# Loading wv and wq by rows, and splitting the first transposed copy between two engines

## The chip, the cores and the metric

The kernel runs on one core of one Trainium2 chip. A core has TensorE (matrix products; its weight loads are listed apart), VectorE, ScalarE, GpSimd, and SyncE (SP), whose queue issues the transfers that sixteen DMA engines carry out. In the profile they are PE, PEld, DVE, ACT, POOL and SP. The metric is device time in microseconds (us), lower is better.

## The reference

The input x has 2048 rows of 512 bf16 values; it is normalised by rows, and that xn feeds two branches:

```
xn  = layernorm(x)
qkv = xn @ wqkv                     # 512 x 1536: q, k and v, 32 heads of 16
s   = attention over 8 positions (pos, pos-2, ..., pos-14) of each head, then @ wo
h   = gelu(layernorm(xn) @ w1); its four column quarters shifted by +1, -1, +2, -2 rows; @ w2
x1  = xn + h
g   = silu(x1 + gelu(layernorm(x1) @ w3) @ w4)
out = x + s * g
```

`wqkv` is one matrix in memory, 1536 columns wide. Its columns 0 to 511 are wq, the next 512 wk, the last 512 wv. A row of one of these three parts is 1024 bytes long and lies 3072 bytes from the next row.

## The kernel before, in words

The rows are taken in two interleaved halves (even and odd rows), each as eight tiles of 128 rows; four tiles make a chunk of 512, so there are four chunks (0 to 3). The weights are held with 128 of their 512 input rows to a block, on the 128 partitions: index `dt` from 0 to 3 runs over these row blocks.

The order of work on each engine is the order of the program text; nothing is reordered, and engines wait for one another by semaphores. SP's queue is one list as well. Its first entries are, in this order: row tiles 0 and 1 (L105, 128 KB each), wv as one transfer (L114, 512 KB), row tiles 2 and 3 (L105), wq as two transfers of 256 of its 512 columns each (L118), wk (L121), then the tiles of chunk 1 two at a time (L105), w1 (L125), the tiles of chunk 2 (L105). A transfer in this list also waits until the one eight places before it has landed, because eight semaphores are used in turn.

The start, which the change touches, goes as follows. VectorE measures each row tile (L225, L227), ScalarE and VectorE make the inverse deviation (L232, L234), VectorE normalises the tile in place (L241). For chunk 0 TensorE then transposes the tiles. Tiles 0 and 1 go one at a time through `turn_one` (four 128 x 128 transposes each, L318, into one PSUM bank, which is copied to `xnT` at L320: tile 0 by VectorE, tile 1 by ScalarE). Tiles 2 and 3 go together through `turn` (L308, copied by VectorE at L309).

TensorE's list from there is: the v products of tiles 0 and 1 (`v_mm`, L380, four per tile, one for each row block of wv); the q products of tiles 0 and 1 for the first 256 columns of wq (`q_half`, L331, eight); the transposes of tiles 2 and 3 (L308); the q products of tiles 0 and 1 for the other 256 columns (eight); then the q products of tiles 2 and 3, eight and eight, with one product for the row factors of the second layer norm between them (`rows2_here`, L291); then k (`k_all`, L341 by way of `proj`), further v tiles, and w1 (L341). In `q_half` the loop over `nt` (four groups of 128 output columns) is the outer one and the loop over `dt` the inner one: a column group is finished before the next is begun. The four groups lie in four PSUM banks.

ScalarE, after tile 1's copy: the square roots for tiles 2 and 3 (L232), for the row factors (L259), the copy of v out of PSUM (L391), the load of another function table (L556, 1.28 us), the copy of the row factors (L292), the two copies of q (L352), then those of k (L371). Banks are used in pairs, three pairs in turn, and two single banks.

The rest is the second and third chunks' projections, w2, w3 (L489), and from about 108 us on an attention part in 18 steps, in which the products with w4 (L819) fill TensorE's list between the attention's own; it ends with the products with wo (L876) and the gates on VectorE (L891, L895).

Of the kernel before, what the change touches and what calls it, by code (L numbers as in the profile page):

```python
# [8 lines left out]
AF = mybir.ActivationFunctionType  # L9
# [11 lines left out]
def kernel(  # L21
# [17 lines left out]
    PE, DVE, ACT, POOL, SP = nc.tensor, nc.vector, nc.scalar, nc.gpsimd, nc.sync  # L39

    def pin(ins):

        return tc.keep_in_program_order(ins)
# [3 lines left out]
    D = 512  # L47
    F = 1376
    ND = D // P
# [20 lines left out]
    wqkv_v = A_wqkv.rearrange("(dt q) n -> q dt n", q=P)  # L70
# [14 lines left out]
    def b4(shape, name):  # L85
        return sm4.tile(shape, BF16, name=name, tag="b4")
# [4 lines left out]
    def pair():  # L91
        cnt["d"] += 1
        b = 2 * ((cnt["d"] - 1) % 3)
        return PS[:, b : b + 2, :]

    def single():
        cnt["s"] += 1
        return PS[:, 6 + (cnt["s"] - 1) % 2, :]
# [4 lines left out]
    def load_x(c, t0, n):  # L103
        p, i = c // 2, (c % 2) * TPC + t0
        pin(SP.dma_start(  # L105
            out=xn[p][:, i : i + n, :], in_=xv[p, i * P : (i + n) * P, :].rearrange("(i q) d -> q i d", q=P)
        ))

    wq_sb = b4([P, ND, D], "wq_sb")
    wk_sb = b4([P, ND, D], "wk_sb")  # L110
    wv_sb = b4([P, ND, D], "wv_sb")
    load_x(0, 0, 1)
    load_x(0, 1, 1)
    pin(SP.dma_start(out=wv_sb, in_=wqkv_v[:, :, 2 * D : 3 * D]))  # L114
    load_x(0, 2, 1)
    load_x(0, 3, 1)
    for h in range(2):
        pin(SP.dma_start(  # L118
            out=wq_sb[:, :, h * D // 2 : (h + 1) * D // 2], in_=wqkv_v[:, :, h * D // 2 : (h + 1) * D // 2]
        ))  # L120
    pin(SP.dma_start(out=wk_sb, in_=wqkv_v[:, :, D : 2 * D]))  # L121
    load_x(1, 0, 2)
    load_x(1, 2, 2)
# [186 lines left out]
            out=xnT[p][:, :, i * P : (i + 2) * P], in_=pt.rearrange("p a j q -> p a (j q)")  # L310
        ))

    def turn_one(c, t, eng):
        p, k = c // 2, c % 2
        i = k * TPC + t
        pt = single().bitcast(BF16)[:, 0 : ND * P].rearrange("p (a q) -> p a q", a=ND)
        for dt in range(ND):
            pin(PE.transpose(pt[:, dt, :], xn[p][:, i, dt * P : (dt + 1) * P], ident[:]))  # L318
        dst = xnT[p][:, :, i * P : (i + 1) * P]
        pin(DVE.tensor_copy(out=dst, in_=pt) if eng is DVE else ACT.activation(dst, pt, AF.Copy))  # L320

    def turn_dma(c, lo=0, hi=TPC):
        p, k = c // 2, c % 2
# [1 line left out]
            i = k * TPC + t  # L325
            pin(SP.dma_start_transpose(out=xnT[p][:, :, i * P : (i + 1) * P], in_=xn[p][:, i, :]))

    def q_half(pts, lo, hi, nts=range(ND)):
        for nt in nts:
            for dt in range(ND):  # L330
                pin(PE.matmul(  # L331
                    pts[nt // 2][:, nt % 2, lo:hi], lhsT=wq_sb[:, dt, nt * P : (nt + 1) * P],
                    rhs=xnT[0][:, dt, lo:hi], start=(dt == 0), stop=(dt == ND - 1),
                ))
# [208 lines left out]
    for t in range(2):  # L543
        l0.root_act(t, t + 1, 1)
        l0.apply(t, t + 1)
    turn_one(0, 0, DVE)
    turn_one(0, 1, ACT)
    pv = pair()
    for t in range(2):
        v_mm(0, t, pv[:, t, :])  # L550
# [5 lines left out]
    pin(ACT.preload_act_table_set("gelu_apprx_tanh_and_others"))  # L556
    pq = [pair(), pair()]
    q_half(pq, 0, 2 * P, (0, 1))
    turn(0, 1)
    rows2_inverse(0)  # L560
    q_half(pq, 0, 2 * P, (2, 3))
    load_x(3, 0, 2)
    load_x(3, 2, 2)
    pin(SP.dma_start(out=w2_sb, in_=B_w2.rearrange("(g q) n -> q g n", q=P)))
    q_half(pq, 2 * P, CH, (0, 1))
    rows2_here(0)
    q_half(pq, 2 * P, CH, (2, 3))
# [46 lines left out]
    while vputs:  # L614
# [23 lines left out]
        out=w4_sb[:, 0 : NF - 1, :],  # L638
        in_=B_w4[0 : (NF - 1) * P, :].rearrange("(ft q) n -> q ft n", q=P),
# [457 lines left out]
```

## Time and profile before

| | us |
|---|---|
| median of three timed runs | 190.67 (190.31 to 190.85) |
| the profiled execution's own time | 192.08 |
| its span, first to last instruction | 190.4 |
| TensorE busy | 181.2 (95% of the span) |
| ScalarE busy | 132.0 (69%) |
| VectorE busy | 116.3 (61%) |
| DMA, share of the sixteen engines (main queue) | 53.5% |
| granted TensorE clock | 1.000 |

How to read it: a line of the timeline or of the groups gives the start, the busy time, engine, line of the kernel, operation, what is written from what, how many, and in brackets the idle time before it with the engine, tile and line that ended it. A line of the chain gives the start, the duration and what held the end at that time. In a table by stretches the columns are the busy times (with the number of instructions) of PE, PEld, DVE, ACT and POOL, then the granted clock, the DMA share and GB/s. A busy TensorE is one that has matmuls in flight; their ends are modelled.

### The profile page before, as it was taken

Reading aid. Unit: us, or ns where it says so; the run is one execution under the profiler, and the core shown is the slowest. Engines: PE = TensorE matmul, PEld = TensorE weight load, DVE = VectorE, ACT = ScalarE, POOL = GpSimd, SP = SyncE. Lnnn points to the kernel's source line nnn. Section 1 sums busy time; section 2 is a strip of 40 time slices with the busy share of each in tenths; the row PEclk is TensorE's granted clock in tenths of the full one; section 3 lists DMA queues with packets and bytes.
Section 4 is the critical chain, followed back from the end, with each engine's and each line's share of the span. In section 5 each row is a group of like instructions: output and inputs, shape, how many; then the busy total and the mean of one; then the engine's idle time right before and its main releaser. Section 6 shows DMA issues by size and latency. Waiting matters only on the chain.

```text
span 190.4 us, 5313 instructions
## 1 busy us (share of the span) xinstructions
PE 181.2 (95%) x2247; PEld 89.5 (47%) x2276; DVE 116.3 (61%) x230; ACT 132.0 (69%) x155; POOL 20.8 (11%) x60
## 2 busy tenths in 40 slices
PE   7899999999999999999999999999999999999991
PEld 2284444444444444444444445454545545454570
DVE  5767785370372896765000044566498889799894
ACT  7279957896249325255587679689768788867982
POOL 3005647000020022043000000000000000000000
PEclk9999999999999999999999999999999999999999
DMA  4999576568803599724610051125542675761236
GB/s 117 322 352 333 91 153 108 104 219 265 301 14 62 135 283 196 142 41 84 205 46 0 0 169 55 59 67 174 161 110 65 169 217 175 191 197 36 78 107 229
DMA packets 39860, 27.75 MB, mean 146 GB/s; under 512 B 18068, under 2 KB 39324, under 8 KB 39836
## 3 DMA queue, kind: packets, MB, share of 16 engines
q1 hardware_dynamic: 39836, 27.41, 53.5%
q8 instruction: 18, 0.29, 0.6%
q14 instruction: 6, 0.05, 0.1%
HBM read 17.14 MB, written 6.59 MB: 125 GB/s over the span
## 4 chain that ended last, share of the span: by engine, by line
PE 88%; DMA 3%; DVE 3%; issue 2%; SPq 1%; ACT 1%
PE PS L819 20%; PE PS L489 18%; PE PS L341 16%; PE PS L445 7%; PE PS L380 6%; PE PS L876 4%; PE PS L850 4%; DMA wq_sb<-in_A_wqkv_dram 3%; PE PS L707 3%; PE PS L681 3%; PE PS L717 2%; PE PS L331 2%; DVE sg L891 1%; PE PS L507 1%; DVE xo L895 1%
## 5 line engine op out<-in xcount | busy, mean ns | idle before, releaser
L489 PE MATMUL PS<-x1nT,w_sb 128*128 128x512 bf16 x157 | 34.9, 379 | 0.2
L688 ACT ACTIVATE prob<-PS 128x1824 bf16<-128x1824 f32 x18 | 30.4, 1687 | 1.6 <-PE PS L681 1.6
L819 PE MATMUL PS<-w_sb,h3a 128*128 128x512 bf16 x111 | 28.9, 379 | 1.5 <-issue 1.1
L832 DVE TENSOR_TENSOR xn<-PS,xn 128x512 bf16<-128x512 f32 x15 | 10.3, 690 | 31.9 <-PE PS L819 31.7
L494 ACT ACTIVATE h3a<-PS 128x1024 bf16<-128x1024 f32 x16 | 16.4, 1024 | 19.1 <-PE PS L489 18.4
L489 PEld LDWEIGHTS <-w_sb 128*128 128x128 bf16 x160 | 15.6, 98 | 19.1 <-issue 0.4
L693 DVE TENSOR_TENSOR prob<-prob,maskb 128x1824 bf16<-128x1824 bf16 x18 | 19.8, 1101 | 1.6 <-ACT prob L688 1.6
L371 ACT ACTIVATE kM<-PS,em 128x1024 bf16<-128x1024 f32 x12 | 16.0, 1401 | 2.3 <-PE PS L341 2.3
L819 PEld LDWEIGHTS <-h3a 128*128 128x128 bf16 x128 | 11.3, 97 | 13.0 <-issue 0.2
L453 DVE TENSOR_TENSOR xn<-PS,xn 128x1024 bf16<-128x1024 f32 x8 | 9.6, 1213 | 12.2 <-PE PS L445 12.2
L876 PE MATMUL PS<-wo_sb,oT 128*128 128x512 bf16 (+1 forms) x80 | 15.5, 336 | 0.0
L380 PE MATMUL PS<-wv_sb,xnT 128*128 128x512 bf16 x62 | 15.0, 382 | 0.2
L883 ACT ACTIVATE sg<-PS 128x512 bf16<-128x512 f32 (+1 forms) x20 | 10.1, 512 | 7.1 <-PE PS L876 6.8
L341 PE MATMUL PS<-xnT,wk_sb 128*128 128x512 bf16 x63 | 14.7, 379 | 0.1
L341 PE MATMUL PS<-xn2T,w_sb 128*128 128x512 bf16 x62 | 14.4, 379 | 0.1
L445 PE MATMUL PS<-w_sb,hT 128*128 128x512 bf16 x63 | 14.3, 379 | 0.1
L819 PE MATMUL PS<-w_sb,h3b 128*128 128x512 bf16 (+1 forms) x45 | 12.9, 380 | 0.9 <-issue 0.8
L418 ACT ACTIVATE hT<-PS 128x1024 bf16<-128x1024 f32 x8 | 8.2, 1030 | 5.3 <-PE PS L341 4.7
L391 ACT ACTIVATE vst<-PS 128x1024 bf16<-128x1024 f32 x8 | 8.1, 1018 | 4.3 <-PE PS L380 2.9
L225 DVE BATCH_NORM_STATS2 l1s<-xn 128x6 f32<-128x512 bf16 x16 | 10.2, 681 | 1.4 <-DMA xn<-in_A_x_dram 1.4
L876 PEld LDWEIGHTS <-oT 128*128 128x128 bf16 x80 | 7.8, 98 | 6.0
L225 DVE BATCH_NORM_STATS2 l3s<-xn 128x6 f32<-128x512 bf16 x16 | 10.2, 682 | 0.2
(112 smaller groups left out, 240.0 us busy)
## 6 DMA issues: line engine op xcount, KB each, us to landing
ring<-v_d SPq DMA_DIRECT2D x18, 256.0 KB, 4.6
v_d<-vst SPq DMA_DIRECT2D x16, 256.0 KB, 2.9
xo<-in_A_x_dram SPq DMA_DIRECT2D x8, 256.0 KB, 3.7
ring<-rec_d SPq DMA_DIRECT2D x8, 228.0 KB, 3.8
out_dram<-xo SPq DMA_DIRECT2D x7, 256.0 KB, 3.0
xn<-in_A_x_dram SPq DMA_DIRECT2D x6, 256.0 KB, 6.2
w_sb<-in_B_w_dram SPq DMA_DIRECT2D x1, 1376.0 KB, 7.8
w_sb<-in_B_w_dram SPq DMA_DIRECT2D x1, 1280.0 KB
```

Of the source, the lines that this page charges most:

```text
L225: pin(DVE.bn_stats(out=self.st[:, j, :], in_=self.src[:, j, :]))
L341: pin(PE.matmul(pt[:, b, :], lhsT=w[:, dt, nt * P : (nt + 1) * P], rhs=rhs[:, dt, :], start=(dt == 0), stop=(dt == ND - 1),))
L371: pin(ACT.activation(dst, pt, AF.Copy, scale=sc))
L380: pin(PE.matmul(pt, lhsT=xnT[p][:, dt, t * P : (t + 1) * P], rhs=wv_sb[:, dt, :], start=(dt == 0), stop=(dt == ND - 1),))
L445: pin(PE.matmul(pt[:, j, :], lhsT=w2_src(p, g, m0), rhs=w2_sb[:, g, :], start=(g == 0), stop=(g == ND - 1),))
L489: pin(PE.matmul(pt[:, b, :], lhsT=w3_sb[:, dt, ft * P : (ft + 1) * P], rhs=x1nT[:, dt, :], start=(dt == 0), stop=(dt == ND - 1),))
L494: pin(ACT.activation(t[:, o : o + 2, :], pt, AF.Gelu_apprx_tanh))
L688: pin(ACT.activation(pr, S_ps[:, :, 0 : ND * NQ], AF.Exp, scale=SCALE))
L693: pin(DVE.tensor_tensor(out=f, in0=f, in1=maskb[:], op=ALU.min))
L819: pin(PE.matmul(pt, lhsT=h3_of(c, ft)[:fs, jj * P : (jj + 1) * P], rhs=w4_sb[:fs, ft, :], start=(ft == 0), stop=(ft == NF - 1 and silu < 2),))
L832: pin(DVE.tensor_tensor(out=x_i, in0=pt, in1=x_i, op=ALU.add))
L876: pin(PE.matmul(pt[:, 0:W], lhsT=oT[p][:, dt, i * P : (i + 1) * P], rhs=wo["sb"][:, dt, c], start=(dt == 0), stop=(dt == ND - 1),))
```

## The change

Four edits in the first microseconds:

- wv is loaded by three transfers: row block 0, row block 1, row blocks 2 and 3 (128, 128 and 256 KB), instead of one.
- wq is loaded in two halves as before, but by rows (row blocks 0 and 1, then 2 and 3, all 512 columns) instead of by columns. A contiguous piece of memory is 1024 bytes instead of 512.
- `q_half` takes row blocks instead of column groups: `dt` is the outer loop and `nt` the inner, so that the first call needs the first half of the rows of wq, and four accumulations are open in four banks at a time.
- `turn_one` gets the number of row blocks that VectorE copies; ScalarE copies the others. Tile 0 is split two and two; tile 1 is ScalarE's alone, as before. In the changed program ScalarE's half of tile 0 carries a wait for VectorE.

```diff
-    pin(SP.dma_start(out=wv_sb, in_=wqkv_v[:, :, 2 * D : 3 * D]))
+    for lo, hi in ((0, 1), (1, 2), (2, ND)):
+        pin(SP.dma_start(out=wv_sb[:, lo:hi, :], in_=wqkv_v[:, lo:hi, 2 * D : 3 * D]))
     load_x(0, 2, 1)
     load_x(0, 3, 1)
     for h in range(2):
-        pin(SP.dma_start(
-            out=wq_sb[:, :, h * D // 2 : (h + 1) * D // 2], in_=wqkv_v[:, :, h * D // 2 : (h + 1) * D // 2]
-        ))
+        pin(SP.dma_start(out=wq_sb[:, 2 * h : 2 * h + 2, :], in_=wqkv_v[:, 2 * h : 2 * h + 2, 0:D]))
...
-    def turn_one(c, t, eng):
+    def turn_one(c, t, split):
...
-        pin(DVE.tensor_copy(out=dst, in_=pt) if eng is DVE else ACT.activation(dst, pt, AF.Copy))
+        if split:
+            pin(DVE.tensor_copy(out=dst[:, 0:split, :], in_=pt[:, 0:split, :]))
+        pin(ACT.activation(dst[:, split:ND, :], pt[:, split:ND, :], AF.Copy))
...
-    def q_half(pts, lo, hi, nts=range(ND)):
-        for nt in nts:
-            for dt in range(ND):
+    def q_half(pts, lo, hi, dts):
+        for dt in dts:
+            for nt in range(ND):
...
-    turn_one(0, 0, DVE)
-    turn_one(0, 1, ACT)
+    turn_one(0, 0, 2)
+    turn_one(0, 1, 0)
```

## The prediction, made before the changed kernel ran

> **What bounds the kernel now.** I read the page's busy table first, then the chain that ended last, then that chain and the timeline for the first 14 us, where all edits lie, and last the DMA rates there.
>
> ```profile
> PE 181.2 (95%) x2247; PEld 89.5 (47%) x2276; DVE 116.3 (61%) x230; ACT 132.0 (69%) x155; POOL 20.8 (11%) x60
> ...
> PE 88%; DMA 3%; DVE 3%; issue 2%; SPq 1%; ACT 1%
> ```
>
> TensorE carries 88% of the chain, so what delays it early is paid at the end. The DMA share is one piece:
>
> ```profile
> 3.22 6.43 DMA wq_sb<-in_A_wqkv_dram
> 9.66 0.05 issue
> 9.71 1.05 PE PS L331 x8
> 10.75 0.45 PE PS L308 x8
> 11.20 1.82 PE PS L331 x16
> ```
>
> The first q products (L331) wait for the first half of wq. Around them:
>
> ```profile
> 6.05 0.42 DVE L320 COPY xnT<-PS 128x512 bf16<-128x512 bf16 x1 [0.18 <-PE PS L318]
> 6.54 2.06 PE L380 MATMUL PS<-wv_sb,xnT 128*128 128x512 bf16 x8
> 6.57 0.60 ACT L320 ACTIVATE xnT<-PS 128x512 bf16<-128x512 bf16 x1 [1.39 <-PE PS L318]
> 6.85 1.29 DVE L225 BATCH_NORM_STATS2 l1s<-xn 128x6 f32<-128x512 bf16 x2 [0.38 <-DMA xn<-in_A_x_dram]
> ...
> 8.92 0.74 DVE L241 TENSOR_SCALAR xn<-xn,l1m,l1r 128x512 bf16<-128x512 bf16 x2
> ...
> 9.71 1.05 PE L331 MATMUL PS<-xnT,wq_sb 128*128 128x256 bf16 x8 [1.11 <-DMA wq_sb<-in_A_wqkv_dram]
> ...
> 11.04 1.98 PE L331 MATMUL PS<-xnT,wq_sb 128*128 128x256 bf16 x16
> ```
>
> TensorE has v (L380) done at 8.60, idles 1.11 us, and starts q at 9.71. Beside that idle time runs a second chain: row tiles 2 and 3 land, are measured (L225), and are normalised by 9.66 (L241); their transposes (L308) come right after the first eight q products. From 9.71 on the table of waits lists none of TensorE's matmuls behind another engine. The DMA rates in half-microsecond stretches:
>
> ```profile
> 3.00:3.50 0.50, 0.50 (x3) 0.15 (x1) 0.35 (x1) 0.50 (x1) 0.00 (x0) 1.00 0.45 78
> 3.50:4.00 0.50, 0.50 (x2) 0.15 (x1) 0.47 (x3) 0.50 (x1) 0.00 (x0) 1.00 0.74 104
> 4.00:4.50 0.50, 0.50 (x2) 0.15 (x1) 0.50 (x2) 0.29 (x1) 0.00 (x0) 1.00 0.74 211
> ...
> 6.50:7.00 0.50, 0.50 (x3) 0.21 (x3) 0.15 (x1) 0.43 (x1) 0.00 (x0) 1.00 0.91 273
> 7.00:7.50 0.50, 0.50 (x4) 0.22 (x3) 0.50 (x2) 0.17 (x1) 0.00 (x0) 1.00 0.74 214
> ...
> 9.00:9.50 0.50, 0.00 (x0) 0.00 (x0) 0.50 (x2) 0.00 (x0) 0.00 (x0) 1.00 1.08 370
> ```
>
> The last column is GB/s: a dip when wv begins (78 to 211), a second while wq's 512-byte pieces move (273, 214), 370 with 1024-byte pieces. The trace also marks when each of the sixteen DMA engines has done its share. Row tile 3: middle 6.54, last 7.28. First wq half: middle 7.42, fifteenth 7.99, last 9.66. So one engine of sixteen makes TensorE wait; it keeps a lag of some 1.7 us through the following loads (second half 8.82 and 10.53, wk 10.32 and 12.04), and gained it just in the 512-byte stretch.
>
> **The change part by part.**
>
> Execution: the profiled run took 192.08 us, span 190.40 and 1.68 around it; the three timed runs have median 190.67, 1.41 under it. I sum in the profiled run and subtract from the median. Whether the timed runs hold the whole 1.11 us of idle time cannot be seen; that is a rival below.
>
> *wv in three pieces.* SP issues two transfers more, at 0.43 us (L114) to 0.51 us each: 0.9 us on SP, which is moved past by row tiles 2 and 3, wq, wk and what follows. Tile 2 would be issued at 3.1 instead of 2.20 and wq's first half at 4.1 instead of 3.22. From issue to first data the first x load needs 0.81 to about 1.9, 1.1 us, so the two could begin at 4.2 and 5.2; the engines reach their bytes only after wv, at about 5.6 and 6.2. The backlog hides the 0.9 us; without it tile 2 and all behind it come up to 0.9 us later. Between the ends 0 and +0.9 I take 0, since SP is 1 us ahead at both places. [...] Each transfer waits for the one eight places before it; both lists move by two from wk on, so the pairs stay.
> For v: wv's last part lands at 6.47, L380 starts at 6.54. The first pieces can only be earlier. Taken as 0 beside the copies.
>
> *The copies of tiles 0 and 1.* Before, VectorE copies tile 0 in 0.42 (L320) and ScalarE tile 1 in 0.60. Now VectorE copies half of tile 0; from 512 elements in 0.42 and 1024 in 0.69 (L309) a half is about 0.29, between 0.21 and 0.42. It ends at 6.34 instead of 6.47: v may start 0.13 earlier. ScalarE's half, in the changed program, waits for VectorE's and not for TensorE directly, so they run one after the other: 6.38 to about 6.77 (0.60 for 512 against 1.02 for 1024 in L352 gives 0.39; at worst 0.60, to 6.98). Behind it on ScalarE is tile 1's copy: 6.77 to 7.37, at worst 7.58, instead of 7.17. Tile 1's first v product is due four products of 0.22 after the start, at 7.4 to 7.6. So v ends 0.15 earlier to 0.05 later, say 0.1 earlier, at 8.50. VectorE's 0.13 buys nothing more: its next work waits for row tile 2 (0.38 idle, L225).
>
> *wq by rows.* The same 512 KB, in 1024-byte pieces, half as many. The 512-byte half took the middle engine 0.88 us (6.54 to 7.42) and the latest 2.38 (7.28 to 9.66). A row load of sixteen 1024-byte pieces per engine shows 0.74 (marks 12.80 and 13.54 of row tiles 4/5 and 6/7). By that the first half lands at 7.28 + 0.74 = 8.0 on the latest engine. At the other end, if its pause has nothing to do with piece size, 9.66 or a little less. I take 8.0: all engines lose rate just there, and the lag grows nowhere else in this burst. The second half lands by 8.8 instead of 10.53; it is needed after the transposes.
>
> *q by row blocks.* Same 32 matmuls on the same four banks, another order: block one is rows 0-1 for all four column groups, which is what the first half holds. TensorE cost 0. Only the first ScalarE copy of q (L352) now waits for the last block, six eighths into it; that copy follows L292, which already comes after, so 0; uncovered, it would be 0.65 (six eighths of 0.87).
>
> **The sum.** With wq in place at 8.0, q starts at 8.50 and its eight products end near 9.4. The transposes then meet the second chain: tile 3 is normalised at 9.66, unchanged. They start 0.06 later and the last four take half of 0.45: q goes on at 9.94 instead of 11.04, gain 1.1. So 1.1 is not the 1.11 by itself: the idle time goes, the 0.1 of the copies goes too, and a wait for VectorE takes back 0.1 to 0.2. Next on ScalarE: its table load ends at 12.46, so L292 starts there instead of 13.28, only 0.82 earlier; but ScalarE then waited 0.17 for TensorE at L371, so from there it is 0.99 earlier. TensorE needs that bank back at 18.92, and L371 is done at 18.54: slack 0.38 falls to 0.27. The next due load, DMA-transposed tiles 4 to 7, lands at 21.08 to 23.86 (kept where it is) for products at 22.75 and later, 1.1 earlier now: still in time by 0.4. So 1.1 goes to the end, at least 0.8 if ScalarE's late table rules instead. I take 1.0: 190.67 - 1.0 = 189.7.
>
> **The rivals.**
>
> *No change: the late engine stays, or the timed runs never had it.* The one trace shows one pause; if it belongs to the engine and not to the pieces, wq lands at about 9.5, gain 0.15 to 0.3. If the timed runs wait for row tile 3 already (9.66), q goes on at 9.94 in both kernels, gain 0. For it: the profiled run is 1.41 longer than the median, and the idle time is 1.11. Against it: the rate dip under 512-byte pieces is common to all engines. 190.5, between 190.3 and 190.8. Chance 0.29.
>
> *Slower: wv's start is paid more than once.* When wv begins, three half-microsecond stretches run at 78, 104 and 211 instead of 370 GB/s: (292 + 266 + 159) x 0.5 / 370 = 0.97 us lost. If each added piece pays that again, row tiles 2 and 3 and all behind them land up to 1.9 us later; tile 3 is normalised at 11.6 and q goes on at 11.9, 0.8 after the present. It decides from 1.1 us of added delay in the profiled picture, and from 0.3 if the timed runs hold no idle time (then up to +1.9). Against it: the second x load, issued 0.46 after the first, has its last mark 0.29 after it (3.13, 3.42), and x, wk and w1 follow each other without a dip. 191.5, between 191.2 and 192.5. Chance 0.27.
> The Trainium skill, "DMA: Bandwidth & Descriptors", section "Rules for kernel authors", speaks against this change: small transfers are to be joined, and section "Anatomy of one DMA" gives each a fixed cost of about 2.0 us; paid in series, an estimate from that page, two more transfers would be 4 us. The 0.29 between the x loads shows that here the fixed part overlaps.
> The same page, "Why small descriptors are slow", has a fixed bus cost per piece; that is 9% between 512 and 1024 bytes by its formula, an estimate, and the dip to 214 is far deeper.
>
> **How the numbers follow.** Faster as summed 0.44, no change 0.29, slower 0.27. The first alone is 189.3 to 190.0 (the upper bound is ScalarE's 0.8 less 0.1; the lower has tiles 2 and 3 landing 0.3 earlier). For eight in ten I leave out the top of the slower case: 189.3 to 191.6. About 0.3%, 0.57 us, is what a measurement of this kernel can tell from none; a gain of 1.0 is over it, the second case inside it.
>
> **What would show it.** After: the wait of L331 for wq gone or under 0.3; L308 waiting for L241 of VectorE instead; the 16 products of L331 starting near 9.9; L225's pair still starting near 6.85; v ending near 8.5; 6.5 to 8.0 us at 330 GB/s or more; the last marks of wq at 8.0 and 8.8. Wrong if one engine's mark for wq still stands at 9.5 (second case), or if L225 starts past 7.5 (third).

## The result: slower by 0.43%, and the profile after

The changed kernel takes 191.47 us (median of seven runs, 191.09 to 192.10), the kernel before on the same chip 190.63 (seven runs, 190.31 to 190.85). The ratio is 1.0043, 95% interval 1.0030 to 1.0055. So the change costs 0.84 us. The forecast was 189.7, a gain. The time lies in the range given, but near its upper end, where the prediction had its rival "slower".

The profiled execution took 192.10 us with a span of 190.2; it is the slowest of the seven, whose spans go from 189.0 to 190.2 (median 189.5). The kernel before, over 115 timed runs taken beside the experiments below, has a median span of 189.1, and eight in ten of its spans lie between 188.9 and 189.8. The execution that the prediction read (190.4) is longer than nearly all of these.

The page of the changed kernel, its busy engines and the shares of the chain that ended last:

```profile
PE 181.0 (95%) x2247; PEld 89.2 (47%) x2276; DVE 116.2 (61%) x230; ACT 132.0 (69%) x156; POOL 20.8 (11%) x60
...
PE 81%; DMA 7%; DVE 4%; SPq 2%; issue 2%; ACT 1%; POOL 1%
```

TensorE has the same work (181.0 against 181.2), but less of the chain, and transfers have more (7% against 3%). The timeline of the start (start, duration, engine, line; L115 is wv, L105 the row tiles, L119 wq, L321 and L322 the copies to `xnT`, L382 v, L333 q, L224 the measuring of a row tile, L240 its normalising, L307 the transposes of tiles 2 and 3):

```profile
1.73 1.38 SPq L115 DMA_DIRECT2D wv_sb<-in_A_wqkv_dram  x3
...
3.15 0.94 SPq L105 DMA_DIRECT2D xn<-in_A_x_dram  x2
...
5.83 0.29 DVE L321 COPY xnT<-PS 128x256 bf16<-128x256 bf16 x1
...
6.15 0.87 ACT L322 ACTIVATE xnT<-PS 128x256 bf16<-128x256 bf16 x2 [0.98 <-DVE xnT L321]
...
6.18 1.94 PE L382 MATMUL PS<-wv_sb,xnT 128*128 128x512 bf16 x8
6.29 0.69 DVE L224 BATCH_NORM_STATS2 l1s<-xn 128x6 f32<-128x512 bf16 x1 [0.17 <-DMA xn<-in_A_x_dram]
...
7.64 0.69 DVE L224 BATCH_NORM_STATS2 l1s<-xn 128x6 f32<-128x512 bf16 x1 [0.65 <-DMA xn<-in_A_x_dram]
...
8.78 1.05 PE L333 MATMUL PS<-xnT,wq_sb 128*128 128x256 bf16 x8 [0.66 <-DMA wq_sb<-in_A_wqkv_dram]
...
9.12 0.73 DVE L240 TENSOR_SCALAR xn<-xn,l1m,l1r 128x512 bf16<-128x512 bf16 x2
...
9.66 0.64 PE L307 MATMUL PS<-ident,xn 128*128 128x128 bf16 x8
...
10.27 1.92 PE L333 MATMUL PS<-xnT,wq_sb 128*128 128x256 bf16 x16
```

Row tile 2 is issued at 3.15 instead of 2.20, 0.95 us later. v starts at 6.18 and ends at 8.12, and then TensorE again waits for wq, 0.66 us, until 8.78. VectorE waits 0.65 us for row tile 3, which lands at 7.62. In the execution that the prediction read the wait for wq was longer (1.11), but the experiments speak against this wait in the timed runs of before. The rates in half-microsecond stretches (the last two columns are the DMA share and GB/s):

```profile
5.00:5.50 0.50, 0.38 (x4) 0.11 (x3) 0.46 (x3) 0.17 (x1) 0.00 (x0) 1.00 0.94 326
5.50:6.00 0.50, 0.38 (x6) 0.20 (x6) 0.50 (x2) 0.00 (x0) 0.00 (x0) 1.00 1.01 236
6.00:6.50 0.50, 0.50 (x6) 0.25 (x6) 0.33 (x2) 0.35 (x2) 0.00 (x0) 1.00 0.82 209
6.50:7.00 0.50, 0.50 (x4) 0.13 (x2) 0.49 (x1) 0.50 (x2) 0.00 (x0) 1.00 0.74 176
7.00:7.50 0.50, 0.50 (x3) 0.21 (x3) 0.00 (x0) 0.03 (x1) 0.00 (x0) 1.00 0.75 242
```

From 5.5 to 7.5 us only 176 to 242 GB/s move, though row tiles 2 and 3, both halves of wq and wk had been issued by 5.6. There is a second place further on. The chain to 24 us (start, duration, what held the end):

```profile
5.63 6.71 DMA xn<-in_A_x_dram
...
16.35 5.85 DMA xnT<-xn
22.20 0.05 issue
22.25 1.90 PE PS L382 x8
```

Row tiles 4 and 5, issued at 5.63, end in DMA-transposed tiles that land at 22.20. TensorE has finished its products before them at 21.92 (16 products from 18.30 in 3.62) and idles 0.33 us. In this execution TensorE thus waits at two places for transfers of the late list, 0.66 us at q and 0.33 us here.

### The profile page after: what moved, and what is told of

It is laid out like the page before. It is cut to its first block, busy times and chain, and to the rows that moved or that the text cites. A ratio compares the mean times of both kernels' runs of the same rounds, so it can differ in the third digit from the quotient of the medians.

```text
span 190.2 us, 5316 instructions
## 1 busy us (share of the span) xinstructions
PE 181.0 (95%) x2247; PEld 89.2 (47%) x2276; DVE 116.2 (61%) x230; ACT 132.0 (69%) x156; POOL 20.8 (11%) x60
## 4 chain that ended last, share of the span: by engine, by line
PE 81%; DMA 7%; DVE 4%; SPq 2%; issue 2%; ACT 1%; POOL 1%
PE PS L821 20%; PE PS L491 18%; PE PS L343 13%; PE PS L447 7%; PE PS L382 6%; PE PS L878 4%; PE PS L852 4%; DMA xn<-in_A_x_dram 4%; PE PS L709 3%; PE PS L683 3%; DMA xnT<-xn 3%; PE PS L719 2%; DVE sg L893 1%; PE PS L509 1%; DVE xo L897 1%
## 5 line engine op out<-in xcount | busy, mean ns | idle before, releaser
L496 ACT ACTIVATE h3a<-PS 128x1024 bf16<-128x1024 f32 x16 | 16.4, 1024 | 19.1 <-PE PS L491 18.4
L382 PE MATMUL PS<-wv_sb,xnT 128*128 128x512 bf16 x62 | 14.9, 380 | 0.5 <-DMA xnT<-xn 0.3
L224 DVE BATCH_NORM_STATS2 l1s<-xn 128x6 f32<-128x512 bf16 x16 | 10.3, 684 | 2.1 <-DMA xn<-in_A_x_dram 2.1
L224 DVE BATCH_NORM_STATS2 l3s<-xn 128x6 f32<-128x512 bf16 x16 | 10.3, 683 | 0.2
```

Of the source, the lines that this page charges most:

```text
L224: pin(DVE.bn_stats(out=self.st[:, j, :], in_=self.src[:, j, :]))
L382: pin(PE.matmul(pt, lhsT=xnT[p][:, dt, t * P : (t + 1) * P], rhs=wv_sb[:, dt, :], start=(dt == 0), stop=(dt == ND - 1),))
L496: pin(ACT.activation(t[:, o : o + 2, :], pt, AF.Gelu_apprx_tanh))
```

## The experiments: which part it is

Unless another base is named, each kernel is the kernel before with the edit shown. "Time" is a median, and "ratio" is to the kernel before on the same chip in the same batch, whose median is 190.89 for the first four runs, 190.82 for the next four, 190.87 for the four after them and 190.99 for the last three.

**wv in three pieces, alone** (e1):

```diff
-    pin(SP.dma_start(out=wv_sb, in_=wqkv_v[:, :, 2 * D : 3 * D]))
+    for lo, hi in ((0, 1), (1, 2), (2, ND)):
+        pin(SP.dma_start(out=wv_sb[:, lo:hi, :], in_=wqkv_v[:, lo:hi, 2 * D : 3 * D]))
```

> Before with wv in three pieces alone. Theory A (the two added transfers push row tiles 2 and 3, wq and all later transfers of SP's list back): most of the change's loss is here, 191.2 to 191.7 against 190.6. Theory B (the rows of wq): the same as before, 190.4 to 190.8. Theory C (the split copy makes ScalarE late): 190.4 to 190.8.

Measured: 191.62 us, ratio 1.0038 (1.0024 to 1.0052). This one edit has the whole loss, to within what is measured. Its chain at the start:

```profile
4.13 4.78 DMA wq_sb<-in_A_wqkv_dram
8.91 0.04 issue
8.95 1.05 PE PS L332 x8
10.00 0.45 PE PS L309 x8
10.45 1.82 PE PS L332 x16
```

The end hangs on SP's list up to wq, issued at 4.13, and then on wq's landing at 8.91.

**wq by rows with q by row blocks, alone** (e2):

```diff
+        pin(SP.dma_start(out=wq_sb[:, 2 * h : 2 * h + 2, :], in_=wqkv_v[:, 2 * h : 2 * h + 2, 0:D]))
...
+        for dt in dts:
+            for nt in range(ND):
```

> Before with wq in row halves and q by row blocks alone. Theory A: not slower, 189.9 to 190.7. Theory B (by rows the four column groups of q all end late, or the half lands later): most of the loss is here, 191.2 to 191.7. Theory C: 190.4 to 190.8.

Measured: 190.69 us, ratio 0.9997 (0.9978 to 1.0016). Neither gain nor loss can be told.

**The split copy, alone** (e3):

```diff
-    turn_one(0, 0, DVE)
-    turn_one(0, 1, ACT)
+    turn_one(0, 0, 2)
+    turn_one(0, 1, 0)
```

> Before with tile 0's copy split between VectorE and ScalarE alone. Theory A and theory B: 190.4 to 190.8, since the copies lie ahead of a wait for wq. Theory C (ScalarE's half waits for VectorE, tile 1's copy follows it, v ends later): 191.2 to 191.7.

Measured: 190.73 us, ratio 0.9995 (0.9971 to 1.0018). Nothing to be seen.

**The changed kernel with wv in one transfer again** (e4, against the changed kernel):

```diff
-    for lo, hi in ((0, 1), (1, 2), (2, ND)):
-        pin(SP.dma_start(out=wv_sb[:, lo:hi, :], in_=wqkv_v[:, lo:hi, 2 * D : 3 * D]))
+    pin(SP.dma_start(out=wv_sb, in_=wqkv_v[:, :, 2 * D : 3 * D]))
```

> The changed kernel with wv in one transfer again. Theory A: the loss is gone, 190.0 to 190.7. Theory B and theory C: the loss stays, 191.2 to 191.7.

Measured: 190.79 us, ratio 0.9996 (0.9984 to 1.0008). Without the pieces the loss is gone, and the other two edits together give nothing. Its timeline (here L381 is v, L332 q, L306 the transposes):

```profile
6.06 1.94 PE L381 MATMUL PS<-wv_sb,xnT 128*128 128x512 bf16 x8
...
7.84 1.04 PE L332 MATMUL PS<-xnT,wq_sb 128*128 128x256 bf16 x8
...
8.88 0.72 PE L306 MATMUL PS<-ident,xn 128*128 128x128 bf16 x8
...
9.44 1.32 PE L332 MATMUL PS<-xnT,wq_sb 128*128 128x256 bf16 x10
```

q follows v without a wait, and the later q products start at 9.44 instead of 10.27. Between 4.5 and 8.0 us 326 to 387 GB/s move in every half microsecond: the fall after 5.5 us is not there.

**The kernel before once more** (e12), no edit, for a second profile.

> The kernel before once more, for a second profile of it. If the late DMA engine of the first profile (wq's first half complete at 9.66 us, TensorE idle for 1.11 us) belongs to that execution alone, its span is 188.7 to 189.5 us and the first q products start at 8.0 to 8.5 us; if it belongs to the kernel, 190.2 to 190.6 and 9.7.

Measured: 190.86 us, ratio 1.0000 (0.9985 to 1.0014). In this profile the start is early, and yet the span is 190.1. The expectation holds for the start and fails for the span. Two places of its timeline:

```profile
8.24 1.04 PE L331 MATMUL PS<-xnT,wq_sb 128*128 128x256 bf16 x8
9.11 0.61 PE L308 MATMUL PS<-ident,xn 128*128 128x128 bf16 x8
9.56 1.04 PE L331 MATMUL PS<-xnT,wq_sb 128*128 128x256 bf16 x8
...
167.93 0.34 PE L681 MATMUL PS<-qT,kM 32*128 32x57 bf16 x21
169.13 0.26 PE L681 MATMUL PS<-qT,kM 32*128 32x57 bf16 x11 [0.86 <-issue]
```

wq's first half is there on all sixteen DMA engines at 7.77 us (against 9.66 in the execution that the prediction read), q starts at 8.24 with no wait, and its later products at 9.56 instead of 11.04. In e3, and in e13 and e15 further down, wq comes in 512-byte pieces as well, and its first half is complete on all engines between 7.76 and 7.99. So the late DMA engine belonged to the one execution, not to the kernel and not to the 512-byte pieces. Most of what makes this second execution long is the 0.86 us of idle time in the middle of 32 products, which the profile puts down to no other engine.

## The experiments: what about the pieces

Two theories were left: the pieces as such (each start of wv's transfer paid again, or smaller pieces moving worse), or the place that two more issues take in SP's list (they use up the lead that SP has over the DMA engines).

**wv whole, two unused loads of 16 KB behind it** (e5):

```diff
     pin(SP.dma_start(out=wv_sb, in_=wqkv_v[:, :, 2 * D : 3 * D]))
+    for i in range(2):
+        pin(SP.dma_start(out=spare[0:16, i, :], in_=xv[1, M - 16 : M, :]))
```

> Before, wv in one transfer, with two unused 16 KB loads issued right behind it: SP's list is 0.9 us later from row tile 2 on and the semaphores in turn move by two, as in the change, but wv is whole. Theory L (the loss is the head start of SP's list that the two added issues use up): 191.3 to 191.8, L331 waits for wq until 8.9 or so. Theory P (the loss is in wv's row pieces as transfers, which make the engines' reads slow): 190.5 to 191.0, L331 starts near 8.0.

Measured: 191.69 us, ratio 1.0036 (1.0015 to 1.0057). As slow as with three pieces, with wv in one. Its chain:

```profile
4.15 4.76 DMA wq_sb<-in_A_wqkv_dram
8.91 0.05 issue
8.95 1.05 PE PS L334 x8
10.00 0.01 issue
10.01 0.72 PE PS L311 x8
10.73 1.82 PE PS L334 x16
```

wq is issued at 4.15 and q starts at 8.95, the same figures as with the pieces (4.13 and 8.95).

**wv in two row pieces** (e6):

```diff
+    for lo, hi in ((0, 2), (2, ND)):
+        pin(SP.dma_start(out=wv_sb[:, lo:hi, :], in_=wqkv_v[:, lo:hi, 2 * D : 3 * D]))
```

> Before with wv in two row pieces, blocks 0-1 and 2-3: one added issue of 0.46 us. Theory L: half the delay, 190.9 to 191.3, unless a first 0.4 us is still covered (then as before). Theory P: between 190.9 and 191.7, with a dip of the DMA rate between 5.5 and 7.5 us as with three pieces.

Measured: 190.95 us, ratio 0.9996 (0.9976 to 1.0016). One issue more, row tile 2 issued 0.50 us later (2.70), costs nothing that can be measured. Yet the rate falls here too, and deeper than in the changed kernel:

```profile
5.00:5.50 0.50, 0.50 (x5) 0.15 (x4) 0.46 (x3) 0.13 (x1) 0.00 (x0) 1.00 1.33 226
5.50:6.00 0.50, 0.38 (x8) 0.20 (x5) 0.50 (x2) 0.00 (x0) 0.00 (x0) 1.00 0.31 97
6.00:6.50 0.50, 0.50 (x6) 0.21 (x5) 0.21 (x1) 0.19 (x1) 0.00 (x0) 1.00 0.58 180
6.50:7.00 0.50, 0.50 (x4) 0.23 (x3) 0.20 (x1) 0.41 (x1) 0.00 (x0) 1.00 1.03 314
...
8.26 1.05 PE L332 MATMUL PS<-xnT,wq_sb 128*128 128x256 bf16 x8
```

It begins earlier and is over by 6.5 us. wq's first half is complete at 8.21, just before TensorE, done with v at 8.17, starts q at 8.26. So a fall of the rate is not yet a loss: in e1 and e5, which lose time, wq's first half is complete at 8.91, long after TensorE could have gone on.

**wv in three pieces by partitions** (e7):

```diff
+    for lo, hi in ((0, 32), (32, 64), (64, P)):
+        pin(SP.dma_start(out=wv_sb[lo:hi], in_=wqkv_v[lo:hi, :, 2 * D : 3 * D]))
```

> Before with wv in three pieces by partitions (32, 32 and 64 of 128, all four row blocks in each), so each piece reads rows out of the whole matrix as the one transfer does. Theory L: as slow as three row pieces, 191.3 to 191.8. Theory P in the form that it is the row blocks being read one after the other: 190.5 to 191.0; in the form that it is the number of wv transfers: 191.3 to 191.8.

Measured: 192.11 us, ratio 1.0057 (1.0033 to 1.0082). SP spends 1.68 us on the three, and row tile 2 goes out at 3.44, 1.24 us late. In its profile TensorE also waits 0.6 us for wv itself, so this run doesn't set pieces and lead apart.

**The three row pieces, the second and third issued by ScalarE's queue** (e8; a clearing is moved from ScalarE to GpSimd to make room):

```diff
+    pin(SP.dma_start(out=wv_sb[:, 0:1, :], in_=wqkv_v[:, 0:1, 2 * D : 3 * D]))
+    for lo, hi in ((1, 2), (2, ND)):
+        pin(ACT.dma_start(out=wv_sb[:, lo:hi, :], in_=wqkv_v[:, lo:hi, 2 * D : 3 * D]))
```

> Before with wv in the same three row pieces, but the second and third issued from ScalarE's queue at its start, so that SP's list is no longer than before; the clearing of the first v buffer goes from ScalarE to GpSimd, which is idle then. Theory L: the loss is gone, 190.4 to 190.9. Theory P: it stays, 191.3 to 191.8.

Measured: 190.92 us, ratio 1.0001 (0.9982 to 1.0020). The three pieces of wv cost nothing here, with no entry added to SP's list. From the lines of both queues:

```profile
0.80 0.91 ACTq L116 DMA_DIRECT2D wv_sb<-in_A_wqkv_dram  x2
...
1.73 0.42 SPq L114 DMA_DIRECT2D wv_sb<-in_A_wqkv_dram  x1
2.19 0.91 SPq L105 DMA_DIRECT2D xn<-in_A_x_dram  x2
3.14 0.98 SPq L120 DMA_DIRECT2D wq_sb<-in_A_wqkv_dram  x2
```

Row tile 2 goes out at 2.19 and wq at 3.14, as in the kernel before (2.20 and 3.22). The Trainium skill, "DMA: Bandwidth & Descriptors", section "Rules for kernel authors", says that spreading transfers over issuing engines brings no bandwidth and saves only the sequencer's issue time. This run agrees as far as the issue time goes: row tile 2 goes out at 2.19 instead of 3.15 (e1), and the ratio falls from 1.0038 to 1.0001. It doesn't change the issue time alone: ScalarE's queue issues its two pieces from 0.80 us on, ahead of SP's first at 1.73, so that three quarters of wv are also asked for earlier than in the other kernels. That the list's lead is what counts is shown by the runs that follow.

**No transfer added: row tile 2's load held back** (e9, e10, e13, e14). GpSimd clears row tile 2's buffer a few times, and SP's list waits at that load. The diff is that of e9; e10 has four clearings, e13 three, e14 three and one of a quarter of the size:

```diff
+    for _ in range(5):
+        pin(POOL.memset(xn[0][:, 2, :], 0.0))
     load_x(0, 2, 1)
     load_x(0, 3, 1)
```

> The kernel before, with no transfer added or split: row tile 2's load on SP's queue waits until some 3.2 us, because GpSimd clears its buffer five times first (0.46 us a clearing from 0.8 us on). SP's list behind it is then 0.9 to 1.0 us late, as with wv in three pieces. Theory L (the list's head start is used up): 191.3 to 191.8 us, the 8 products of the first half of q from some 8.9 us on in the profile instead of 8.0, and a fall of the moved GB/s between 5 and 7 us. Theory P (it is the number of transfers): 190.6 to 191.0, q as before. Whether the time outside the span stays at some 1.7 us (no transfer more) or is 1.9 to 2.1 as in the kernels with two transfers more is told beside it.

> As the last, with four clearings: the list is 0.5 to 0.6 us late, as with wv in two pieces. Theory L with a head start of 0.5 to 0.9 us: 190.7 to 191.1 us, the same as before within what is measured. If the head start were less, or the loss grew in proportion to the delay, 191.1 to 191.4.

> The kernel before with row tile 2's load held back by three clearings on GpSimd: it starts at some 2.77 us instead of 2.20, 0.57 us late. If the start covers at least that, 190.7 to 191.0 us; if the cover ends near the 0.47 us that wv in two pieces cost nothing for, 191.0 to 191.4.

> As the last with a short fourth clearing: some 0.75 us late. If the loss sets in as a step between 0.57 and 0.9 us, 191.4 to 191.8 us or as before; if it grows in proportion from the end of the cover, 191.0 to 191.4.

The first two were held longer than meant: GpSimd's clearings came 0.6 to 0.8 us apart at first, not 0.46, with other work of GpSimd between them. Row tile 2 was issued at 3.92 and 3.34 us, 1.72 and 1.14 late. So the expectations for e9 and e10 were written for delays that they didn't have. All delays in order, with the two kernels above that shift the list by issues; "outside" is the time less the span:

| kernel | row tile 2 issued | late by | time | ratio | span | outside |
|---|---|---|---|---|---|---|
| before | 2.20 | 0 | 190.8 to 191.0 | 1 | 189.1 | 1.73 |
| e6, two pieces | 2.70 | 0.50 | 190.95 | 0.9996 | 189.1 | 1.80 |
| e13, three clearings | 2.76 | 0.56 | 190.96 | 1.0004 (0.9985 to 1.0024) | 189.15 | 1.80 |
| e14, and a short one | 3.02 | 0.82 | 191.18 | 1.0007 (0.9990 to 1.0024) | 189.4 | 1.78 |
| e1, three pieces | 3.15 | 0.95 | 191.62 | 1.0038 | 189.65 | 1.94 |
| e5, two unused loads | 3.21 | 1.01 | 191.69 | 1.0036 | 189.7 | 1.99 |
| e10, four clearings | 3.34 | 1.14 | 191.75 | 1.0043 (1.0020 to 1.0066) | 190.0 | 1.74 |
| e9, five clearings | 3.92 | 1.72 | 191.87 | 1.0053 (1.0034 to 1.0072) | 190.15 | 1.76 |

A pure delay makes the loss, and three clearings of the same buffer make none (e13), so what costs is the lost lead of SP's list and not the clearings. The lead covers about 0.6 us, within the 0.2% that e6 and e13 can tell; from 0.8 us on the median span rises, by some 0.3 at 0.82, 0.55 at 0.95 and 0.9 at 1.14, and then flattens. e14's own interval still holds no change; only its span speaks for a beginning of the loss. From the timelines of the shortest and the longest delay, e13 first:

```profile
2.76 0.81 SPq L105 DMA_DIRECT2D xn<-in_A_x_dram  x2
...
8.25 1.04 PE L331 MATMUL PS<-xnT,wq_sb 128*128 128x256 bf16 x8
```

and e9:

```profile
3.92 0.81 SPq L105 DMA_DIRECT2D xn<-in_A_x_dram  x2
...
9.20 1.05 PE L333 MATMUL PS<-xnT,wq_sb 128*128 128x256 bf16 x8 [0.81 <-DMA wq_sb<-in_A_wqkv_dram]
```

With 0.56 us of delay q starts at 8.25 with no wait, as in the kernel before (8.24). With 1.72 it waits 0.81 us for wq, and the rate between 5.0 and 7.0 us is 171 to 244 GB/s, a fall like that of the changed kernel with no transfer added.

**Two unused loads far down SP's list** (e15), behind the row tiles of chunk 2, so that nothing at the start moves:

```diff
     load_x(2, 2, 2)
+    for i in range(2):
+        pin(SP.dma_start(out=spare[0:16, i, :], in_=xv[1, M - 16 : M, :]))
```

> The kernel before with two unused loads of 16 KB far down SP's list, behind the loads of the third chunk, where SP is well ahead: nothing at the start moves. If an entry of SP's list costs 0.1 us outside the span, the time less the span is 1.9 to 2.1 us instead of 1.7 and the time 190.9 to 191.2 us; if not, 1.7 and 190.7 to 191.0.

Measured: 190.99 us, ratio 0.9986 (0.9966 to 1.0005), median span 188.95, outside it 1.98. The time as a whole is not shown to differ, but the part outside the span is 0.25 us longer than before (1.73, between 1.67 and 1.85 in all 115 runs; here 1.91 to 2.08). It is so in all the kernels here with two entries more in SP's list (e1, e5, e7, the changed kernel: medians 1.94 to 1.99), and in none with a pure delay or with the two entries on ScalarE's queue (1.74 to 1.80). So of the changed kernel's 0.84 us some 0.24 lie outside the span (1.97 against 1.73). The other 0.6 within it is a difference; the median spans themselves, 189.5 and 189.1, come from different batches and are 0.4 apart.

**A shorter list** (e11, against e4):

```diff
-    load_x(0, 2, 1)
-    load_x(0, 3, 1)
+    load_x(0, 2, 2)
```

> The changed kernel with wv in one transfer and row tiles 2 and 3 in one transfer as well: SP's list is one entry and 0.45 us shorter than before. Theory L: the head start was enough already, so 190.5 to 191.0 us; a gain of up to 0.3 us if an earlier list still helps. Against it: row tile 2 then lands with row tile 3, some 0.3 us later, and if the start hangs on it the time is 191.0 to 191.3.

Measured: 191.23 us, ratio 1.0015 (1.0001 to 1.0030): 0.4 us more than e4, in another batch. wq is issued 0.47 us earlier, but row tile 2 now lands with row tile 3: VectorE's measuring starts at 6.63 instead of 6.34, the transposes at 9.16 instead of 8.88, the later q products at 9.72 instead of 9.44. The start hangs on row tile 2 there, not on SP. The Trainium skill, "DMA: Bandwidth & Descriptors", section "Rules for kernel authors", advises joining small transfers into one, and calls those under 64 KB mostly overhead; these are of 128 KB, and joining them did not pay, because VectorE had begun with the first tile (landed at 6.32 in e4) where it now waits for both (6.60).

No version was found that beats the kernel before.

## Why the prediction was wrong, point by point

- *"The backlog hides the 0.9 us ... Between the ends 0 and +0.9 I take 0, since SP is 1 us ahead at both places."* This step failed. The pieces did make SP 0.95 us late, but the cover is about 0.6 us, not 1.0: with the list late by 0.56 the kernel loses nothing that can be told, late by 0.95 to 1.14 it loses 0.55 to 0.9 of span. The working took the time from issue to first data from the very first load and let the engines go straight from wv, at full rate, to the next transfer. In the changed kernel the rate falls to 176 to 242 GB/s for two microseconds after wv instead, row tile 3 lands at 7.62 and the first half of wq at 8.73, against 6.63 and 7.77 in the second profile of before, and TensorE waits 0.66 us at q. The term stood at 0 in the sum; it measures some 0.6 us in the span.
- *The execution.* The prediction noted that it could not see whether the timed runs hold the whole 1.11 us of idle time, and made it a rival. They don't: the second profile of before starts q at 8.24 and goes on at 9.56, where the forecast for the changed kernel was 9.94. So the other term that failed is the gain: 1.0 us was reckoned from one late DMA engine in one execution, and the part of the change that was to bring it brings nothing (e2 0.9997; e4, with everything but the pieces, 0.9996). The sign was in hand, that execution's time of 192.08 against a median of 190.67: 1.41 us more, of which the wait is 1.11.
- *wq by rows.* That 1024-byte pieces move faster is not shown: between 6.5 and 8.0 us e4 moves 354 to 365 GB/s and e3, which has columns, 292 to 319, but e2, which has rows, only 252 to 287. Nor do rows rule out a late engine: in e2 the second half of wq is complete on fifteen engines at 8.95 and on the last at 9.46. wq's halves were complete at 8.73 and 10.23, not 8.0 and 8.8, because of the late list. Alone the edit is worth nothing (0.9997), because usual executions don't wait for wq (q starts without a wait in e3, e12, e13 and e15).
- *The copies.* ScalarE's half does run behind VectorE's, as read from the changed program: VectorE's 0.29 us as reckoned, then ScalarE from 6.15 on with its two copies in 0.87. The 0.1 us by which v was to end earlier can't be told from nothing (0.9995). v ended at 8.12 instead of 8.50, but e15, without the split, starts it at 6.20 and the changed kernel at 6.18, so this difference is not shown to be the split's.
- *q by row blocks* at nothing: right (in the 0.9997).
- *The later loads.* DMA-transposed tiles 4 to 7 were "kept where it is", landing from 21.08. They landed from 22.20, and TensorE idled 0.33 us for them. Row tiles 4 and 5 are in the same late list: they land at 12.35, the transposing transfers go out at 16.35, against 10.42 and 15.31 in e4, with wv whole, where the transposed tiles land from 20.65. The figure of 21.08 was read where these transfers, issued late (16.91), took 4.17 us; in the changed kernel they take 5.85, in e4 5.34 and in e12 5.49.
- *The sum.* It had no term for the time outside the span. The changed kernel, with two entries more in SP's list, spends 0.24 us more there.
- *The rivals.* "Slower" came true in time (191.5 forecast, 191.47 measured) and at the point given, 0.3 us where the timed runs hold no idle time. Its mechanism did not, so that the figure was met is luck. wv's start is not paid again: the three pieces are all there by 5.94 us, where the one transfer of e12 is there by 5.90, and a list held back with wv whole makes the loss as well (e9, e10). The fixed cost of about 2.0 us that the prediction takes from the Trainium skill, "DMA: Bandwidth & Descriptors", section "Anatomy of one DMA", is given there for transfers issued by GpSimd; those here are issued by SP. "No change" named rightly why the gain isn't there: by e12 and by the times of e2 and e4, the timed runs don't hold the idle time. In e12 v, q, the transposes and the other q products follow each other on TensorE with no wait between them.
- *What would show it.* Of the signs for a gain none came but the early end of v: q waited 0.66 us for wq, went on at 10.27 and not near 9.9, and 176 to 291 GB/s moved between 6.5 and 8.0 us. The sign for the slower case came halfway: the pair of L225 came apart (L224 in the changed kernel), its first instruction at 6.29, even before 6.85, its second at 7.64, past 7.5.

Still open is why the rate falls so far. Some packets in flight are then slow: single packets take up to 1.17 us between 5 and 6 us in the changed kernel, 0.95 in e1, 1.12 in e5, and none over 0.40 in e4 between 4 and 8 us. But e6, which loses nothing, has packets of up to 1.10 us too, and in e9, which loses most of the delayed kernels, none takes over 0.67 between 4 and 8 us. So neither the fall nor the slow packets go with the lateness alone: the list is late by 0.50 in e6 and by 0.56 in e13, and e13 has no fall (279 to 387 GB/s between 4.5 and 8.0 us). What holds the packets isn't in the trace, and no run tried it. Nor is it shown what the 0.24 us outside the span consist of.

## What to carry to other kernels

Before a gain is reckoned from an idle time, set the time of the profiled execution beside those of the others, and take a second profile where it is longer: a wait for one late DMA engine may belong to that execution alone, and the second execution may be long for another reason, as e12 was. An issue added to SP's list here cost its issue time (0.43 to 0.5 us) in lead for everything behind it, and the lead should be measured, by holding the list back by known amounts, rather than read as the distance between issue and first use. Where pieces are wanted for an early start, try issuing the added ones from another queue, as here from ScalarE's, which cost nothing that could be measured.

## What was not expected of the hardware

- One DMA engine of sixteen was late by 1.7 us in one profiled execution of the kernel before (9.66 against 7.99 for the fifteenth) and by nothing to speak of in the second (7.77 against 7.75).
- TensorE stood still for 0.86 us in the middle of 32 like products (168.27 to 169.13 us in e12) with no semaphore that the profile names. This one pause is as long as the whole effect studied here (0.84).
- Two small loads more in SP's list lengthen the time outside the span by 0.25 us, at the start of the list (e5) as further down (e15). Two pieces of wv more on ScalarE's queue don't (e8, 1.74).
- The rate at which the loads move can fall to 97 GB/s for half a microsecond and cost nothing (e6).
